# P times V of every fourth key tile as three f16 products: a fused attention and gated feed-forward kernel on one core

## The chip, the core and the metric

The kernel runs on one core of a Trainium2 chip. A core has five engines that run their own instruction streams and meet at semaphores: PE (TensorE, matrix products; its weight loads, PEld, are recorded apart), DVE (VectorE), ACT (ScalarE), POOL (GpSimd) and SP (SyncE, which here issues the DMAs). Products are written to PSUM, of which the kernel uses eight tiles of 128 x 512 f32 (banks); everything else lies in SBUF. The metric is the time of one execution in microseconds (us), the median of several runs.

## The reference

One block of an adaptive-layernorm transformer, S = 2048 rows, D = 512, 32 heads of 16, one shared key and value head, feed-forward width 1792, all in f32:

```python
mod = silu(c) @ w_mod                      # six rows of 512: sa, ca, ga, sb, cb, gb
h = layernorm(x) * (1 + ca) + sa
q = (h @ wq) as 32 heads of 16;  k = h @ wk;  v = h @ wv
p = softmax(q k^T / 4);  o = p @ v
x = x + ga * (o @ wo)
h = layernorm(x) * (1 + cb) + sb
x = x + gb * (((h @ w_gate) * (h @ w_up)) @ w_down)
```

## The kernel before, in words

**f32 through f16.** Most f32 matrices are kept as two f16 halves, hi and lo, with t = hi + lo: `hi` is t converted, `lo` is t - hi. A product of two such matrices is three f16 products, hi*hi, lo*hi and hi*lo (`TERMS`). Before the change, P times V is the one large product that is still done in f32.

**Tiling.** The rows are cut into 8 blocks of 256 (`ST`), the heads into 4 groups of 8 (`NC`). A block with a head group is a *unit* (`u`, 0 to 31; four units are one *superblock* `sb` of rows). The keys are cut into 16 tiles of 128 (`kt`). For a unit and a key tile, four tiles P of 128 keys x 512 (two heads' queries each, numbered by `p` and `a`) come from four score products (`qk_exp`, L648) and four exponentials on ACT (L661). `pv` (L665) multiplies them with the key tile's V, 128 x 32 (16 values, 16 ones that give the softmax's denominator), as four f32 products side by side in four column groups of 32. This is a *burst*. All 16 key tiles of a unit add up in one PSUM bank, which `pv_out` (L673) evicts. Then `normalise` (L681) brings the sums back over DMAs, and Pool multiplies (L706) and splits the result (L708, L709) for the output projection.

**The maxima.** The softmax needs each row's maximum before its exponentials. For the next unit, score products (L601) go to PSUM and DVE reduces them (L605), 64 a unit.

**The side work.** All other matrix products are *side groups* (`Group`, L511): query projections, output projection (`wo_work`), gate and up (`ffn_work`, 14 groups a superblock, 24 halves of two 256-column products each) and down (2 groups, 84 halves each). A half uses 64 of the 128 rows of PE, so it runs beside a score or maximum product on the other 64 rows. A gate-up group is finished by ACT (`g`, L847), DVE (`gf`, L849) and Pool, which writes the two halves of `glu` (L850, L851).

**The order.** Nothing is scheduled by a planner: `attend` (L1218) writes the program out in turns, two turns for two key tiles. In the side-work style `MANY` a turn is

```python
MANY = "x1 e0 x1 m0 x1 e0 x1 e0 x1 m0 x1 m0 x1 m0 x1 e0"
```

x a side half, e a score product with its exponential, m a maximum product. In the first of the two turns e makes the tiles with `a` = 0 of both key tiles, in the second those with `a` = 1. `end_turn` (L1229) closes a turn: it emits the finishing of side groups that ended in it, the eviction of a unit, then the burst of the key tile before, then `hooks` (L1278), which steps the weight preparation and, at four places of a unit (`NORM_AT`), the normalisation. On each engine the instructions stand in the order in which they are written there.

The two row halves of a side group add into one PSUM bank, so a half may only follow a half of the other rows when that one is done. The program ensures it with a wait of the first half of a turn for the last exponential of the turn before, on ACT (`sync`).

Of the kernel before, what the change touches and what calls it, by code (L numbers as in the profile page):

```python
# [23 lines left out]
ST = 256  # L24
# [10 lines left out]
SLOTS = (0, 1, 2, 3, 6, 7)  # L35
# [5 lines left out]
NORM_AT = (5, 12, 15, 19)  # L41
NBANK = 8
QPRE = 24
# [20 lines left out]
def adaln_mqa_glu_kernel(ctx: ExitStack, tc: tile.TileContext, x_in, wq_in, wk_in, wv_in, wo_in,  # L64
# [37 lines left out]

    c4 = consts.tile([KC, 128], F32, name="c4")
# [11 lines left out]
    for i in range(6, 8):  # L115
        xts.append([work.tile([128, D], F32, name="P", tag="P", bufs=8) for _ in range(2)])
# [12 lines left out]
    hf3 = [work.tile([128, BT], F32, name="P", tag="P", bufs=8) for k in range(KC)]  # L129
# [96 lines left out]
    ssqs = [kwb[:, 2 * n * BT:2 * n * BT + 2 * F].bitcast(F32) for n in (KC, 2 * KC)]  # L226
    kng = kwb[:, 2 * NHF * BT:2 * NHF * BT + BT]
# [86 lines left out]
    def v_mm(b):  # L314
        p = ps_hold("pvt", (128, 4, 16))
        for i in range(4):
            nc.tensor.matmul(p[:, i, :], parts[b][:, i * 128:(i + 1) * 128], lane[:, 16:32], start=True, stop=True)

        def out():
            nc.scalar.activation(vst[:, 4 * b:4 * b + 4, 0:16], p, AF.Copy, scale=inv[:, 0:1] if b else 1.0)  # L320
            ps_give(p)
        posts.append(out)
# [48 lines left out]
    kb = consts.tile([128, 8], F32, name="kb")  # L371
    inv = consts.tile([128, 3], F32, name="inv")
# [15 lines left out]
    nc.gpsimd.tensor_scalar(sckb, sck, inv[:, 0:1], 0.0, op0=OP.mult, op1=OP.add)  # L388
    combine(0, selk)
# [9 lines left out]
    evs = consts.tile([128, 1], F32, name="evs")  # L399

    def ev_scales():

        t = work.tile([128, 2], F32, name="evt", bufs=1)
        nc.vector.tensor_reduce(evs, ident.rearrange("p (a r) -> p a r", a=4)[:, :, 0:16], axis=AX.XY, op=OP.add)
        nc.vector.reciprocal(t[:, 0:1], kb[:, 5:6])
        nc.gpsimd.tensor_tensor(t[:, 0:1], t[:, 0:1], evs, op=OP.mult)
        nc.gpsimd.tensor_scalar(t[:, 1:2], evs, -1.0, 1.0, op0=OP.mult, op1=OP.add)
        nc.gpsimd.tensor_tensor(evs, t[:, 0:1], t[:, 1:2], op=OP.add)

# [43 lines left out]
    def last_rows():  # L453
# [21 lines left out]
             15: lambda: h_halves(1, KA), 17: lambda: h_halves(1, KB), 20: ev_scales}  # L475
# [6 lines left out]
    sync = {"due": False, "exp": None, "before": None}  # L482
    pending = []

    def flush():
        for f in pending:
            f()
            sync["due"] = True
        pending.clear()

    class Group:
# [31 lines left out]
        def half(self, r):  # L523

            mm = self.put(r, r + 1)
            if self.rows not in (None, r):
                tc.add_manual_dep(mm.ins, sync["before"], SYNC)
            self.rows, self.turn, sync["due"] = r, now[0], True
            if self.ended():
                ended.append(self)  # L530
# [89 lines left out]
    def max_fin(u):  # L620
        mms[u] = work.tile([128, 2, 8], F32, name="mm")
        nc.vector.tensor_reduce(mms[u], mparts[u], axis=AX.X, op=OP.max)

# [18 lines left out]
    pvb = {}  # L642
    ptl = {}
    oc = {}
# [3 lines left out]
    def qk_exp(u, kt, p, a, last=False):  # L648
        s = sst[u % 3]
        ptl[u, kt, p, a] = work.tile([128, D], F32, name="P", tag="P", bufs=8)  # L650
        t = ps_sc()
        keys = kst[64 * a:64 * a + 50, kt * 128:(kt + 1) * 128]
        if pending and last:
            for c in range(2):
                if c:
                    flush()
                nc.tensor.matmul(t[:, c * ST:(c + 1) * ST], keys, s[64 * a:64 * a + 50, c, p, :], start=True, stop=True)  # L657
        else:
            nc.tensor.matmul(t.rearrange("k (c n) -> k c n", c=2), keys, s[64 * a:64 * a + 50, :, p, :],  # L659
                             start=True, stop=True)  # L660
        ex = nc.scalar.activation(ptl[u, kt, p, a], t, AF.Exp)  # L661
        if sync["due"]:
            sync.update(due=False, exp=ex.ins.name)

    def pv(u, kt):  # L665
        if kt == 0:
            pvb[u] = ps_hold("pv")
        for j in range(4):
            p, a = divmod(j, 2)
            nc.tensor.matmul(pvb[u][32 * j:32 * j + 32, :], vst[:, kt, :], ptl[u, kt, p, a],  # L670
                             start=(kt == 0), stop=(kt == KT - 1))

    def pv_out(u):  # L673
        sb, ch = divmod(u, NC)
        ev = work.tile([128, BT], F32, name="ev", tag="ev", bufs=3)
        nc.scalar.activation(ev, pvb[u], AF.Copy, scale=evs)
        ps_give(pvb[u])
        pd[u] = dram.tile([128, BT], F32, name=f"pd{u}")
        nc.sync.dma_start(pd[u], ev)
# [48 lines left out]
    def load_x(t):  # L728
        if t < KT - 2:
            x1s[t] = work.tile([128, D], F32, name="x1", tag="x1", bufs=6)  # L730
        else:
            x1s[t] = work.tile([128, D], F32, name="x1p", tag="P", bufs=8)
        nc.sync.dma_start(x1s[t], x_rows[t * 128:(t + 1) * 128, :])
# [58 lines left out]
    def ln2_work(sb):  # L792
        st = {}

        def tr(i):
            def f():
                if not h2s:
                    h2T = big.tile([128, 2, 2, KC, ST], F16, name="h2T", tag="wq")
                    glus.append(big.tile([128, 2, 2, FT, ST], F16, name="glu", tag="big"))
# [32 lines left out]
    def ffn_work(sb):  # L832

        def glu():
            return glus[0][:, sb % 2]
# [57 lines left out]
    def late_weights():  # L893
# [37 lines left out]
        def stage(n):  # L931
            if "d" in W:
                t = work.tile([128, D], F32, name="wsl", tag="xl", bufs=3)
            else:
                t = hfs[:, SLOTS[taken[0] % len(SLOTS)], :]
# [237 lines left out]
    side = deque(wlist)  # L1173
# [43 lines left out]

    def attend(u, kt):  # L1218
# [7 lines left out]
        orders = [[(w[0], int(w[1:] or 0)) for w in s.split()] for s in (style if style is NO_SIDE else (style, style))]  # L1226
        count = {}

        def end_turn(kt):  # L1229
# [3 lines left out]
            for f in ends:  # L1233
                f()
            ends.clear()
# [11 lines left out]
        for turn in range(2):  # L1247
            now[0] = u * NSTEP + 2 * (kt + turn)
            sync["before"] = sync["exp"]
            drain_posts()  # L1250
            order = orders[turn]
            for j, (what, a) in enumerate(order):
                if j == len(order) // 2:
                    drain_posts()
                    if style is not NO_SIDE:
# [22 lines left out]
    def hooks(u, i):  # L1278
# [5 lines left out]
        if u > 0 and i in NORM_AT:  # L1284
            if i == NORM_AT[0]:
                nrm[:] = normalise(u - 1)
            nrm[NORM_AT.index(i)]()
        if i == 20 and u > 0 and u % NC == 0:
# [25 lines left out]
    pv(u, KT - 1)  # L1314
    pv_out(u)
# [61 lines left out]
```

## Time and profile before

| | |
|---|---|
| median of 3 runs | 1664.51 us (1664.37 to 1664.66) |
| span of the profiled execution | 1663.8 us |
| instructions recorded | 39821 |
| attention, first to last burst | 79.5 us to 1551.2 us (starts) |
| after it, the rest of the side work and the last superblock | to 1663.8 us |

The profile is of one execution. Its page gives busy times by engine, the chain of work that ended last, and groups of instructions: a line of the kernel, engine, operation, what it writes and reads, shape and count, then busy time and mean ns of one, then the idle time ahead of it and what ended that. L511 is line 511 of the kernel before. The trace also gives instructions in order of time, with start and duration in us; neighbours of one kind are merged there (x4), and what an engine waited for stands in brackets. Stretches of time give for each engine the busy us and the number of instructions.

### The profile page before, as it was taken

How to read it: one execution, taken by the hardware profiler on the slowest of the kernel's cores; microseconds unless marked ns; L12 is line 12 of the kernel's file. 1: busy time of each engine (PE TensorE's matmuls, PEld its weight loads, DVE VectorE, ACT ScalarE, POOL GpSimd, SP SyncE). 2: the span in 40 equal slices, each digit the busy share in tenths (PEclk: the TensorE clock that was granted, in tenths of full speed). 3: DMA queues.
4: the chain of work that ended last, by engine and by line, in shares of the span. 5: the costliest groups of instructions: out<-in, count | busy, mean ns of one | idle time of the engine just before them, and what ended most of it. 6: DMA issues, size and time to landing. Idle time of an engine off the chain costs nothing.

```text
span 1663.8 us, 39821 instructions
## 1 busy us (share of the span) xinstructions
PE 1643.3 (99%) x15677; PEld 747.1 (45%) x15677; DVE 1402.3 (84%) x2434; ACT 1234.8 (74%) x2389; POOL 523.5 (31%) x833
## 2 busy tenths in 40 slices
PE   8899999999999999999999999999999999999999
PEld 4333333355533554335543355434545345454776
DVE  7999999998998999899998999999998999980211
ACT  5688888888777877777877787777878777877300
POOL 4857537864841111301112011300113001210322
PEclk9999999999999999999999999999999999999999
DMA  6313313342210001000000000000000000000100
GB/s 237 108 59 100 95 43 120 96 129 80 77 51 24 18 12 32 19 32 20 20 26 23 25 13 24 26 25 26 20 29 15 26 22 20 26 14 21 33 13 14
DMA packets 66024, 75.39 MB, mean 45 GB/s; under 512 B 17702, under 2 KB 46634, under 8 KB 65836
## 3 DMA queue, kind: packets, MB, share of 16 engines
q1 hardware_dynamic: 63724, 72.26, 13.7%
q8 instruction: 123, 2.02, 0.5%
q10 hardware_dynamic: 2112, 0.59, 0.1%
q14 instruction: 65, 0.53, 0.1%
HBM read 55.51 MB, written 17.04 MB: 44 GB/s over the span
## 4 chain that ended last, share of the span: by engine, by line
PE 93%; ACT 2%; DVE 2%; DMA 1%; issue 1%; POOL 0%; SPq 0%; ACTq 0%; DVEq 0%
PE side L511 41%; PE pv L670 30%; PE mx L601 8%; PE sc L659 8%; PE sc L657 3%; ACT P L661 2%; DVE mpart L605 1%; DMA xbig<-in_A_x_dram 1%; PE mx L805 1%; PE mxt L629 0%; ACT hf L813 0%; PE sc L601 0%; DVE bs L248 0%; DMA kwb<-in_B_w_down_dram 0%; DMA wkv<-in_A_wv_dram 0%
## 5 line engine op out<-in xcount | busy, mean ns | idle before, releaser
L605 DVE TENSOR_REDUCE mpart<-mx 128x1 f32<-128x512 f32 x2016 | 1274.1, 684 | 104.0 <-PE mx L601 95.7
L661 ACT ACTIVATE P<-sc 128x512 f32<-128x512 f32 x2048 | 1094.8, 598 | 274.2 <-PE sc L659 226.9
L601 PE MATMUL mx<-kst,sst 48*128 48x512 f16 x2032 | 631.5, 377 | 3.8 <-ACT P L661 1.7
L659 PE MATMUL sc<-sst,kst 50*128 50x512 f16 x1792 | 597.5, 379 | 0.6 <-ACT P L661 0.3
L670 PE MATMUL pv<-P,vst 128*32 128x512 f32 x4096 | 545.3, 605 | 0.7
L511 PE MATMUL side<-h2T,wg 64*128 64x256 f16 (+1 forms) x2396 | 540.8, 271 | 0.1
L511 PE MATMUL side<-h2T,wu 64*128 64x256 f16 (+1 forms) x2396 | 538.7, 270 | 0.0
L511 PEld LDWEIGHTS <-wg 64*128 64x128 f16 (+1 forms) x2396 | 226.0, 94 | 230.5 <-ACT P L661 194.0
L511 PE MATMUL side<-wd,glu 64*128 64x512 f16 (+1 forms) x1172 | 272.8, 378 | 0.2 <-ACT P L661 0.2
L850 POOL TENSOR_SCALAR glu<-gf 128x256 f16<-128x256 f32 x112 | 45.8, 409 | 671.3 <-DVE gf L849 583.9
L511 PEld LDWEIGHTS <-wu 64*128 64x128 f16 (+1 forms) x2396 | 226.4, 94 | 43.0 <-issue 7.8
L601 PEld LDWEIGHTS <-sst 48*128 48x128 f16 x2064 | 189.9, 94 | 34.2 <-issue 17.4
L659 PEld LDWEIGHTS <-kst 50*128 50x128 f16 x1792 | 162.9, 94 | 63.0 <-issue 50.3
L511 PEld LDWEIGHTS <-glu 64*128 64x128 f16 (+1 forms) x1172 | 98.5, 94 | 192.4 <-ACT P L661 85.9
L670 PEld LDWEIGHTS pv<-P,vst 128*32 128x32 f32 x4096 | 80.7, 108 | 160.9 <-issue 150.1
L849 DVE TENSOR_TENSOR gf<-side,g 128x256 f32<-128x256 f32 x112 | 46.7, 418 | 79.8 <-ACT g L847 77.7
L657 PE MATMUL sc<-sst,kst 50*128 50x256 f16 x512 | 96.9, 268 | 0.1
L511 PE MATMUL side<-h,wq 64*128 64x512 f16 (+1 forms) x372 | 95.0, 376 | 0.4 <-ACT P L661 0.4
L847 ACT ACTIVATE g<-side 128x256 f32<-128x256 f32 x112 | 42.3, 379 | 65.6 <-PE side L511 65.3
L511 PE MATMUL side<-wo,och 64*128 64x512 f16 (+1 forms) x360 | 86.3, 377 | 0.0
L851 POOL TENSOR_TENSOR glu<-gf,glu 128x256 f16<-128x256 f32 x112 | 75.3, 673 | 9.3
L706 POOL TENSOR_TENSOR oc<-oc,rr 128x256 f32<-128x256 f32 x31 | 22.7, 731 | 146.6 <-DMA rr<-ri 100.4
(233 smaller groups left out, 865.4 us busy)
## 6 DMA issues: line engine op xcount, KB each, us to landing
pd<-ev SPq DMA_DIRECT2D x32, 256.0 KB
kwb<-in_B_w_gate_dram SPq DMA_DIRECT2D x32, 224.0 KB
kwb<-in_B_w_up_dram SPq DMA_DIRECT2D x32, 224.0 KB
sst<-qd SPq DMA_DIRECT2D x180, 32.0 KB
qd<-q SPq DMA_DIRECT2D x16, 256.0 KB
oc<-pd SPq DMA_DIRECT2D x64, 64.0 KB
rr<-ri SPq DMA_DIRECT2D x64, 64.0 KB
x<-in_A_x_dram SPq DMA_DIRECT2D x14, 256.0 KB
```

The source lines that it names most:

```text
L511: return nc.tensor.matmul(self.p[:, c * w:(c + 1) * w], left[rows], right[rows], start=start and c == 0, stop=stop and c == len(terms) - 1)
L601: nc.tensor.matmul(m, s[64 * a:64 * a + 48, t // 2, p, t % 2 * 128:(t % 2 + 1) * 128], w[64 * a:64 * a + 48, :], start=(i == 0), stop=(i = ...
L605: nc.vector.tensor_reduce(part, m, axis=AX.X, op=OP.max)
L657: nc.tensor.matmul(t[:, c * ST:(c + 1) * ST], keys, s[64 * a:64 * a + 50, c, p, :], start=True, stop=True)
L659: nc.tensor.matmul(t.rearrange("k (c n) -> k c n", c=2), keys, s[64 * a:64 * a + 50, :, p, :], start=True, stop=True)
L661: ex = nc.scalar.activation(ptl[u, kt, p, a], t, AF.Exp)
L670: nc.tensor.matmul(pvb[u][32 * j:32 * j + 32, :], vst[:, kt, :], ptl[u, kt, p, a], start=(kt == 0), stop=(kt == KT - 1))
L706: eng.tensor_tensor(o, o, st["r"], op=OP.mult)
L847: nc.scalar.activation(g, p[:, 0:ST], AF.Copy, scale=2.0 ** -45)
L849: nc.vector.tensor_tensor(gf, p[:, ST:2 * ST], g, op=OP.mult)
L850: nc.gpsimd.tensor_scalar(glu()[:, 0, f, :], gf, 1.0, 0.0, op0=OP.mult, op1=OP.add)
L851: nc.gpsimd.tensor_tensor(glu()[:, 1, f, :], gf, glu()[:, 0, f, :], op=OP.subtract)
```

## The change

1. From unit 9 on (when the weight preparation on Pool, `side_items`, has run out), every fourth key tile (`EVERY`) is marked in `split_p`, but for the last two of each superblock's first unit and the first of its second. 76 key tiles are marked.
2. The four P tiles of a marked key tile are written by ACT to a region of their own (`p_split`), and Pool makes the f16 halves of each with a conversion and a subtraction (`p_halves`). They are emitted one P tile at a time: at the end of the key tile's first turn, in the middle and at the end of its second, and in the middle of the next turn. V of these key tiles is split once (`v16`).
3. The burst of a marked key tile comes two turns later than it did (`P_LAG`) and holds twelve f16 products in place of four f32 ones.
4. So that each turn still has one burst, one ready key tile is held back (`ready_p`): the order of key tiles in a unit's sum changes, one turn in unit 9 has no burst, and one burst is left for the end.
5. Ahead of the last exponential of a turn with an f16 burst, ACT makes a 1x1 copy that waits for the last side half; the next turn waits for that copy instead of the exponential.
6. P is scaled by 2^14 for the range of f16 (`P_BIAS` is taken off the maxima by a new 128x16 DVE instruction), V's scale is applied when V is evicted, and the eviction of a unit no longer scales (`evs` is gone).
7. Room: twelve P buffers in place of eight; `glu` has one buffer in place of two; four new P buffers and the split region lie behind it. Two staging slots move (`SLOTS`). The normalisation's places are counted from the unit's eviction (`out_at`).

```diff
-SLOTS = (0, 1, 2, 3, 6, 7)
+SLOTS = (0, 1, 2, 3, 12, 13)
-NORM_AT = (5, 12, 15, 19)
+NORM_AT = (2, 9, 12, 16)
+EVERY = 4
+P_LAG = 2
...
     def max_fin(u):
         mms[u] = work.tile([128, 2, 8], F32, name="mm")
         nc.vector.tensor_reduce(mms[u], mparts[u], axis=AX.X, op=OP.max)
+        nc.vector.tensor_scalar(mms[u], mms[u], -P_BIAS, None, op0=OP.add)
...
+        if (u, kt) in split_p:
+            ptl[u, kt, p, a] = None, p_split[0][:, 2 * a + p]
+            todo_p.append((p, a))
...
+        if last and sync["early"]:
+            ex = nc.scalar.activation(tok[:, 1:2], tok[:, 0:1], AF.Copy)
+            tc.add_manual_dep(ex.ins, sync["half"], SYNC)
+            sync.update(due=False, exp=ex.ins.name)
...
+    def p_halves():
+        if todo_p:
+            p, a = todo_p.popleft()
+            t, (hi, lo) = p_split[0][:, 2 * a + p], [p_split[1][:, 2 * a + p, h] for h in range(2)]
+            nc.gpsimd.tensor_scalar(hi, t, 1.0, 0.0, op0=OP.mult, op1=OP.add)
+            nc.gpsimd.tensor_tensor(lo, t, hi, op=OP.subtract)
...
     def pv(u, kt):
...
+        if (u, kt) in split_p:
+            terms = [(v16[:, vl, kt // EVERY, :], [p_split[1][:, 2 * a + p, pl] for p, a in heads])
+                     for vl, pl in ((0, 0), (1, 0), (0, 1))]
+        else:
+            terms = [(vst[:, kt, :], [t for _, t in parts])]
+        for n, (v, ps) in enumerate(terms):
+            for j in range(4):
+                nc.tensor.matmul(pvb[u][32 * j:32 * j + 32, :], v, ps[j], start=start and n == 0,
+                                 stop=stop and n == len(terms) - 1)
...
+    def split_due(v):
+        return bool(late_p) and v - late_p[0] >= P_LAG
+
+    def pv_turn(v):
+        if divmod(v, KT) in split_p:
+            late_p.append(v)
+        else:
+            ready_p.append(v)
+        if split_due(v):
+            pv(*divmod(late_p.popleft(), KT))
+        elif ready_p:
+            pv(*divmod(ready_p.popleft(), KT))
...
         def glu():
-            return glus[0][:, sb % 2]
+            return glus[0]
...
+        calm = not (u % NC == 0 and kt >= KT // 2 or u % NC == 1 and kt == 0)
+        if style is MANY and kt % EVERY == 0 and p_split and not side_items and calm:
+            split_p.add((u, kt))
...
         def end_turn(kt):
             for g in ended:
                 g.finish()
...
+            p_halves()
             v = u * KT + kt - 1
             if v >= 0:
-                pv(*divmod(v, KT))
-                if v % KT == KT - 1:
-                    ends.append(lambda: pv_out(u - 1))
+                pv_turn(v)
```

How the order of instructions moves. First PE at a turn's end while gate-up groups run: the last score product of the turn, the burst, and the first side half of the next turn. Before (`vst` is V in f32):

```order
L657 MATMUL sc<-sst_130,kst 128x256
L670 MATMUL pv<-P,vst 32x512 x3
L670 MATMUL pv<-P,vst 32x512 [waits Activation_49]
L511 LDWEIGHTS wg [waits Activation_49]
L511 MATMUL side<-h2T,wg 128x256
```

In the changed kernel, at the burst of a marked key tile (`v_341` is `v16`, `glu` the tensor in which the split region lies; the rows left out are the products in between, with a weight load each):

```order
L672 MATMUL sc<-sst_128,kst 128x256
L708 LDWEIGHTS v_341
L708 MATMUL pv<-glu,v_341 32x512 [waits Pool_49]
...
L708 MATMUL pv<-glu,v_341 32x512
...
L708 MATMUL pv<-glu,v_341 32x512 [waits Pool_49]
L512 LDWEIGHTS wg [waits Activation_49]
L512 MATMUL side<-h2T,wg 128x256
```

The burst now waits for Pool at its first, second, fourth and twelfth product, and the side half behind it for ACT as before (for the 1x1 copy).

Second, Pool while gate-up groups run. Before, it has one pair of instructions for a gate-up group, and one normalisation a unit:

```order
L850 TENSOR_SCALAR glu<-gf 128x256 [waits DVE_49]
L851 TENSOR_TENSOR glu<-gf,glu 128x256 [waits Pool_49]
L706 TENSOR_TENSOR oc<-oc,rr 128x256 [waits DMAHW3_49,DMAHW4_49,DMAHW1_49,DMAHW0_49]
L708 TENSOR_SCALAR och<-oc 128x256 [waits PE_49,Pool_49]
L709 TENSOR_TENSOR och<-oc,och 128x256 [waits Pool_49]
```

In the changed kernel the pairs of the split (L688, L689) stand between them:

```order
L913 TENSOR_SCALAR glu<-gf 128x256 [waits DVE_49]
L914 TENSOR_TENSOR glu<-gf,glu 128x256 [waits Pool_49]
L688 TENSOR_SCALAR glu<-glu 128x512 [waits Activation_49]
L689 TENSOR_TENSOR glu<-glu 128x512 [waits Pool_49]
L688 TENSOR_SCALAR glu<-glu 128x512 [waits Activation_49,Pool_49]
L689 TENSOR_TENSOR glu<-glu 128x512 [waits PE_49,Pool_49]
L913 TENSOR_SCALAR glu<-gf 128x256 [waits DVE_49]
L914 TENSOR_TENSOR glu<-gf,glu 128x256 [waits Pool_49]
L688 TENSOR_SCALAR glu<-glu 128x512 [waits Activation_49]
```

The two pairs in the middle are the third and fourth of a marked key tile, behind a gate-up group that ended in its second turn; the pair that begins in the last row is the first of the next marked key tile, behind a group that ended in its first turn.

Third, Pool in the second unit of a superblock, where the layernorm's rows are normalised on Pool (`n`, L769 before, L822 now). Before, the two stand behind their variances with a gate-up product and a normalisation between; now the second one stands between the third and the fourth pair of a marked key tile:

```order
L688 TENSOR_SCALAR glu<-glu 128x512 [waits Activation_49,Pool_49]
L689 TENSOR_TENSOR glu<-glu 128x512 [waits Pool_49]
L822 TENSOR_SCALAR n_18264<-x_17849,st_18018,ry 128x512
L688 TENSOR_SCALAR glu<-glu 128x512 [waits Activation_49,Pool_49]
L689 TENSOR_TENSOR glu<-glu 128x512 [waits PE_49,Pool_49]
```

More of the change, by code (lines that the diff above doesn't have):

```diff
@@ L100, in ps_misc, with p_tile @@
         return ps_mx("misc", shape)
+    def p_tile(n):
+        return work.tile([128, D], F32, name="P", tag=f"P{n}", bufs=1)
     c4 = consts.tile([KC, 128], F32, name="c4")
@@ L115, in adaln_mqa_glu_kernel @@
     for i in range(6, 8):
-        xts.append([work.tile([128, D], F32, name="P", tag="P", bufs=8) for _ in range(2)])
+        xts.append([p_tile(2 * (i - 6) + t) for t in range(2)])
     wqst = [work.tile([128, D], F32, name="wqst", tag="gf", bufs=4) for k in range(KC)]
@@ L128, in adaln_mqa_glu_kernel @@
         nc.sync.dma_start(wqst[k], wq_in[k * 128:(k + 1) * 128, :])
-    hf3 = [work.tile([128, BT], F32, name="P", tag="P", bufs=8) for k in range(KC)]
+    hf3 = [p_tile(4 + k) for k in range(KC)]
     wq = big.tile([128, 2, KC, D], F16, name="wq", tag="wq")
@@ L481, in adaln_mqa_glu_kernel @@
     ended = []
-    sync = {"due": False, "exp": None, "before": None}
+    sync = {"due": False, "exp": None, "before": None, "half": None, "early": False}
     pending = []
@@ L527, in half @@
                 tc.add_manual_dep(mm.ins, sync["before"], SYNC)
-            self.rows, self.turn, sync["due"] = r, now[0], True
+            self.rows, self.turn, sync["due"], sync["half"] = r, now[0], True, mm.ins.name
             if self.ended():
```

96 lines of the change are left out of this document (65 added, 31 removed).

## The prediction

> **What bounds the kernel now.** I read the page's busy shares and its chain of waits first, then the stretches of 100 us, then single turns in order of time, last the groups by line.
>
> ```profile
> PE 1643.3 (99%) x15677; PEld 747.1 (45%) x15677; DVE 1402.3 (84%) x2434; ACT 1234.8 (74%) x2389; POOL 523.5 (31%) x833
> ...
> PE 93%; ACT 2%; DVE 2%; DMA 1%; issue 1%; POOL 0%; SPq 0%; ACTq 0%; DVEq 0%
> ```
> ```profile
> core 0: 1663.8 us, clock 0.998
> ```
> ```profile
> 1000.00:1100.00 100.00, 99.85 (x1020) 45.84 (x1016) 91.92 (x156) 78.86 (x152) 22.91 (x40) 1.00 0.08 23
> 1100.00:1200.00 100.00, 99.96 (x1005) 44.44 (x1005) 91.95 (x155) 78.45 (x150) 10.02 (x18) 1.00 0.07 23
> ```
>
> The columns of the stretches are PE, PEld, DVE, ACT, POOL, then the granted clock. PE is never idle, at full clock, and the chain runs along it for 93%; DVE, at 92%, is next; Pool has 77 to 90 us of every 100 free. A busy PE is not yet a PE that cannot be quicker, so I look at single turns (one turn: 8 halves of a side group, 4 maxima, 4 scores, one burst of P times V):
>
> ```profile
> 999.65 0.28 PE L511 MATMUL side<-h2T,wg 64*128 64x256 f16 x1
> 999.77 0.27 PE L511 MATMUL side<-h2T,wu 64*128 64x256 f16 x1
> ...
> 1000.08 2.25 ACT L661 ACTIVATE P<-sc 128x512 f32<-128x512 f32 x4 [0.65 <-PE sc L659]
> ...
> 1001.56 0.16 PEld L670 LDWEIGHTS pv<-P,vst 128*32 128x32 f32 x8 [0.21 <-issue]
> 1001.56 1.06 PE L670 MATMUL pv<-P,vst 128*32 128x512 f32 x8
> 1002.23 0.38 ACT L847 ACTIVATE g<-side 128x256 f32<-128x256 f32 x1
> 1002.56 0.28 PE L511 MATMUL side<-h2T,wg 64*128 64x256 f16 x1
> ...
> 1002.75 0.42 DVE L849 TENSOR_TENSOR gf<-side,g 128x256 f32<-128x256 f32 x1
> ...
> 1003.25 0.40 POOL L850 TENSOR_SCALAR glu<-gf 128x256 f16<-128x256 f32 x1 [7.46 <-DVE gf L849]
> 1003.74 0.67 POOL L851 TENSOR_TENSOR glu<-gf,glu 128x256 f16<-128x256 f32 x1
> ...
> 1004.41 1.06 PE L670 MATMUL pv<-P,vst 128*32 128x512 f32 x8
> ...
> 1007.26 1.06 PE L670 MATMUL pv<-P,vst 128*32 128x512 f32 x8
> ...
> 1010.18 1.06 PE L670 MATMUL pv<-P,vst 128*32 128x512 f32 x8
> ```
>
> Bursts start 2.85, 2.85 and 2.92 apart. A burst holds PE 1.00 (1001.56 to 1002.56), the sixteen 256-column products of the side group at 0.11 each the other 1.85. PE sets the turn, and whatever stops PE inside a burst is paid in full.
>
> **The change part by part.** *The burst.* A burst holds four f32 products side by side, each recorded as two (4096 for 2048):
>
> ```profile
> L670 PE MATMUL pv<-P,vst 128*32 128x512 f32 x4096 | 545.3, 605 | 0.7
> L670 PEld LDWEIGHTS pv<-P,vst 128*32 128x32 f32 x4096 | 80.7, 108 | 160.9 <-issue 150.1 <-ACT P L661 9.9 <-DVE mpart L605 0.4
> L659 PE MATMUL sc<-sst,kst 50*128 50x512 f16 x1792 | 597.5, 379 | 0.6 <-ACT P L661 0.3
> ```
>
> A recorded half is about 0.22 longer than an f16 product of the same 512 columns, so it streams twice and the burst is four streams of 0.22; the remaining 0.13 of its 1.00 is entry and exit. As three f16 rounds it is 0.78. The order of the instructions has 76 such bursts (912 f16 products), so 76 x 0.218 = 16.6 us are saved if nothing waits. Bounds: 0 (below, third rival) to 0.34 a burst (entry and exit vanish too), 0 to 26 us. I take 0.218; four heads' streams at f16 move as many bytes per us as at f32.
>
> The eight weight loads of the f32 burst lie in its first 0.16 us, under its first round. The Trainium skill ("TensorE: Matmul & The Clock Gate", Part 3, the mechanism) says that a weight load overlaps running products only where their row groups differ, which here they do not; by that rule the loads of rounds two and three would stand in the open and the gain be near nothing. This trace disagrees, with that 0.16.
>
> *Pool's split.* Each of a split key tile's four P tiles takes one conversion and one subtraction, 128x512, of the kinds in the first two rows:
>
> ```profile
> L818 POOL TENSOR_SCALAR h2T<-hf 128x512 f16<-128x512 f32 x14 | 8.6, 617 | 35.3 <-ACT hf L813 31.5 <-PE side L511 3.8
> L819 POOL TENSOR_TENSOR h2T<-hf,h2T 128x512 f16<-128x512 f32 x14 | 16.3, 1163 | 1.2
> L769 POOL TENSOR_SCALAR n<-x,st,ry 128x512 f32<-128x512 f32 x8 | 16.7, 2084 | 0.0
> ```
> ```profile
> 1073.90 0.62 POOL L818 TENSOR_SCALAR h2T<-hf 128x512 f16<-128x512 f32 x1
> 1074.60 1.17 POOL L819 TENSOR_TENSOR h2T<-hf,h2T 128x512 f16<-128x512 f32 x1
> ...
> 1237.23 0.23 POOL L210 TENSOR_SCALAR rv<-st 128x1 f32<-128x1 f32 x1 [11.59 <-DVE st L760]
> ...
> 1239.02 0.19 POOL L215 TENSOR_TENSOR ry<-ry,rt 128x1 f32<-128x1 f32 x1
> ```
>
> With 0.08 between instructions a pair is 1.95, a key tile 7.8 us, 593 us over 76 key tiles. In four turns (11.4 us) Pool has room: 7.8, and 1.24 every third turn for the gate-up product (0.40 + 0.67, two gaps). But Pool works in order, and the burst has a due time. Count from B, the start of the burst that ends the split key tile's first turn. Its f16 burst stands three turns on, at B+8.55; its last round begins 0.44 later, and the last product needs the fourth tile's low half at B+8.99. The first two exponentials end at B-0.9 and B-0.4 (the ACT row: 1000.08, four in 2.25), and for the other two heads at B+2.0 and B+2.5. Pool could thus be ready at B-0.9+7.8 = B+6.9. What spoils this is the gate-up product, which ends every third turn and, as its rows show, can start on Pool only at B+1.69 of its turn (1003.25 against 1001.56), after g and gf; in Pool's order it stands ahead of the split's instructions that follow it. Key tiles come every fourth turn, so in 12 turns three cases occur:
> - it ends in the split's first turn: all four pairs start behind it, at B+1.69+1.24 = B+2.93, and end at B+10.7; PE waits 1.7.
> - in the second turn: two pairs behind it, from B+4.54+1.24 = B+5.78 to B+9.7; PE waits 0.7.
> - in the third: nothing, as the four pairs are ahead of it.
>
> That is 2.4 us lost for 0.65 gained per 12 turns of gate-up work. In the down and output projections nothing is lost. I walked Pool's whole order for all 76 with these prices (other rows at their means, each row no earlier than its operand): 37 in time, 16 late by 0.4 to 0.9 (10 us together), 18 by 1.4 to 1.9 (30), and 5 in the units in which a block's rows are normalised, where L769's 2.08 or the variance chain (L210 to L215, 1.98) stands between a split's pairs, by 2.9 to 4.7 (20). Sum 60 us. Bounds: with pairs 10% shorter the same walk gives 38; with pairs at what half as many columns cost (L850, L851: 1.24 with gaps), 7.
>
> What is queued behind PE's wait: the whole next turn. ACT and DVE then catch up, and turns of 2.92 return to 2.85 for a turn or two: 39 stalls x 0.1 = -4 us.
>
> *The 1x1 copy on ACT* ahead of the last exponential of an f16 turn. It lets the next turn's products go before that exponential ends.
>
> ```profile
> L634 ACT ACTIVATE mt<-mxt 16x128 f16<-16x128 f32 x32 | 8.5, 267 | 15.0 <-PE mxt L629 15.0
> L622 DVE TENSOR_REDUCE mm<-mpart 128x16 f32<-128x64 f32 x32 | 7.0, 220 | 1.1
> ```
> ```profile
> PEld mx L956 <- POOL kwb L946: 2.5, 1, 2.5
> ```
>
> At most 0.27 x 76 = 20 us of ACT, covered by its 0.65 idle at each turn's start; uncovered, the saving would shrink by as much. DVE's new 128x16 subtraction (32 times; L622, the nearest row, takes 0.22) lies in its 8% idle; uncovered 7 us.
>
> *The reserve* lets one turn early in unit 9 go without a burst and puts one burst behind the last turn: -0.3 (that turn is left to DVE, 92% busy) and +1.0. The later normalisation moves with its data. Single glu buffer: the down products that read it precede the writes on PE, 0. Staging slots and the value scales (units 0 to 8): 0, where PE's longest wait for staged weights is that 2.5 us; at most it is gone. Twelve P buffers instead of eight: 0.
>
> Sum, against the profiled execution: 1663.8 - 16.6 + 60 - 4 + 1 = 1704.2. The median of the runs lies 0.7 above the span, so **1705 us**.
>
> **The rivals.**
> 1. *Pool keeps pace* (the other side): no stall, only the gain, 1664.5 - 16.6 + 1 = 1649. It decides where a pair falls to (8.99 - 2.93)/4 = 1.51 us. For it: the profile's page warns that Pool's spans are rough, and Pool's mean load leaves room. Against: the spacing of L818 and L819 is made of start times, and the conversions are the same size and type.
> 2. *Half the stalls*: pairs of about 1.6 us (the walk's stalls then equal the gain), or gate-up products that arrive earlier because the stalls give ACT and DVE time. The time would be 1664.
> 3. *The f16 burst is no shorter*: two more sets of weight loads in the open, 2 x 0.11 a burst as L670's loads are 0.11 each, or DVE at 92% keeps the turn at 2.85. 16.6 us are lost beside the stalls: 1721. The 0.16 above speaks against it. By the rule of the Trainium skill named above, this one comes.
> That the change does not do what it says is excluded by the order of instructions.
>
> **How the numbers follow.** Forecast 0.68, first rival 0.15, second 0.07, third 0.10. The forecast's own range, from the stall sum of 38 to 65 us and the gain's bounds, is 1683 to 1718. Holding 8 in 10 needs the second rival and most of the third: 1660 to 1720. A measurement here tells 0.2%, 3.3 us. Faster: the first rival and a part of the second, 0.17; within 0.2%: 0.05; slower: forecast, third rival and the rest, 0.78.
>
> **What would show it.** In the profile after: f16 bursts of 0.78 where Pool is early; where a gate-up product precedes the four pairs, a PE wait for Pool's L689 of about 1.7 inside the burst, and 0.7 where it stands between them; some 55 to 60 us of such waits in all; Pool's rows L688 and L689 at 617 and 1163 ns. Wrong, if these rows are clearly shorter, if bursts start on time with PE not waiting for Pool, or if the f16 bursts take 1.00 in stages without gate-up work.

## The result: 2.7% slower

The changed kernel takes 1709.33 us (median of 4 runs, 1707.82 to 1711.67), the kernel before 1664.59 (4 runs). The ratio is 1.0267, 95% interval 1.0254 to 1.0280. The profiled execution has a span of 1709.8 us against 1663.8, so 46.0 us are to be explained.

The page of the changed kernel, its busy shares and its chain of waits:

```profile
PE 1654.8 (97%) x15981; PEld 757.2 (44%) x15981; DVE 1410.4 (82%) x2465; ACT 1235.8 (72%) x2465; POOL 1063.2 (62%) x1442
...
PE 84%; POOL 6%; DVE 5%; ACT 3%; issue 2%; DMA 1%; POOLq 0%; ACTq 0%; SPq 0%; DVEq 0%
```

Pool's busy time has doubled from 523.5 us, and Pool, which had no share in the chain, has 6% of it (some 100 us). The same two stretches as before (PE, PEld, DVE, ACT, POOL, granted clock) show PE with gaps, and a clock that is no longer full:

```profile
1000.00:1100.00 100.00, 97.33 (x1078) 49.31 (x1073) 92.56 (x160) 77.83 (x156) 56.06 (x79) 1.00 0.07 22
1100.00:1200.00 100.00, 98.11 (x945) 39.92 (x946) 87.79 (x146) 75.33 (x152) 73.86 (x91) 0.98 0.07 22
```

The groups of the f16 bursts and of Pool's pairs (busy us, mean ns, then the idle time before them and its releaser):

```profile
L689 POOL TENSOR_TENSOR glu<-glu 128x512 f16<-128x512 f32 x304 | 352.6, 1160 | 25.3
L688 POOL TENSOR_SCALAR glu<-glu 128x512 f16<-128x512 f32 x304 | 188.7, 621 | 111.0 <-ACT glu L680 66.4
L708 PE MATMUL pv<-glu,v 128*32 128x512 f16 x912 | 80.8, 385 | 31.1 <-POOL glu L688 15.6
```

The 912 f16 products are there, the pairs cost what their nearest rows said (617 and 1163), and PE stood 31 us inside the bursts. (That is less than the bursts' lengthening below: a recorded product lasts 0.38 us where the next round may follow 0.22 after its start, so the first part of a gap looks busy. A burst's length shows the gap whole.)

A late burst of the kind that the prediction called its first case, in order of time:

```profile
561.27 0.41 POOL L913 TENSOR_SCALAR glu<-gf 128x256 f16<-128x256 f32 x1 [3.96 <-DVE gf L912]
561.76 0.67 POOL L914 TENSOR_TENSOR glu<-gf,glu 128x256 f16<-128x256 f32 x1
562.40 0.62 POOL L688 TENSOR_SCALAR glu<-glu 128x512 f16<-128x512 f32 x1
...
568.25 0.62 POOL L688 TENSOR_SCALAR glu<-glu 128x512 f16<-128x512 f32 x1
568.96 1.16 POOL L689 TENSOR_TENSOR glu<-glu 128x512 f16<-128x512 f32 x1
```
```profile
568.22 0.40 PE L708 MATMUL pv<-glu,v 128*32 128x512 f16 x3
568.92 0.62 PE L708 MATMUL pv<-glu,v 128*32 128x512 f16 x8 [0.31 <-POOL glu L688]
570.16 0.38 PE L708 MATMUL pv<-glu,v 128*32 128x512 f16 x1 [0.62 <-POOL glu L689]
570.47 0.28 PE L512 MATMUL side<-h2T,wg 64*128 64x256 f16 x1
```

The burst before it began at 559.6. Pool waits 3.96 us for the gate-up operand with the split's first tiles behind it, starts the product 1.7 after that burst's start, as forecast, then four pairs without a gap. PE begins at 568.22, does three products, and stands for the fourth tile's two halves. The burst lasts 2.25 (568.22 to 570.47) instead of 0.76.

I measured all 76 f16 bursts so, from their first product to PE's next other product: 39 take 0.76 to 0.81; 14 take 1.05 to 1.40; 17 take 1.59 to 2.39; 5 take 3.42 to 4.78. The 76th is the kernel's last. It is on time too: two f32 bursts stand directly behind it, and the first of them begins 0.66 after it. So 40 are on time. Over 0.76 the late ones have 7.3, 23.7 and 17.9, together 48.9 us.

### The profile page after: what moved, and what is told of

The parts are those of the page before. It is cut to its first block, busy times and chain, and to the rows that moved or that the text cites. A ratio compares the mean times of both kernels' runs of the same rounds, so it can differ in the third digit from the quotient of the medians.

```text
span 1709.8 us, 41661 instructions
## 1 busy us (share of the span) xinstructions
PE 1654.8 (97%) x15981; PEld 757.2 (44%) x15981; DVE 1410.4 (82%) x2465; ACT 1235.8 (72%) x2465; POOL 1063.2 (62%) x1442
## 4 chain that ended last, share of the span: by engine, by line
PE 84%; POOL 6%; DVE 5%; ACT 3%; issue 2%; DMA 1%; POOLq 0%; ACTq 0%; SPq 0%; DVEq 0%
PE side L512 38%; PE pv L708 26%; PE mx L602 8%; PE sc L674 8%; DVE mpart L606 4%; POOL glu L689 3%; PE sc L672 3%; POOL glu L688 2%; ACT P L680 1%; ACT glu L680 1%; DMA xbig<-in_A_x_dram 1%; PE mx L868 1%; PE mxt L631 0%; DVE bs L255 0%; PE sc L602 0%
## 5 line engine op out<-in xcount | busy, mean ns | idle before, releaser
L680 ACT ACTIVATE P<-sc 128x512 f32<-128x512 f32 x1281 | 707.7, 599 | 143.9 <-PE sc L674 104.3
L680 ACT ACTIVATE glu<-sc 128x512 f32<-128x512 f32 x767 | 429.7, 596 | 158.4 <-PE sc L674 113.7
L708 PE MATMUL pv<-P,vst 128*32 128x512 f32 x2562 | 454.9, 606 | 0.7
L689 POOL TENSOR_TENSOR glu<-glu 128x512 f16<-128x512 f32 x304 | 352.6, 1160 | 25.3
L708 PE MATMUL pv<-glu,vst 128*32 128x512 f32 x926 | 303.1, 605 | 0.2
L688 POOL TENSOR_SCALAR glu<-glu 128x512 f16<-128x512 f32 x304 | 188.7, 621 | 111.0 <-ACT glu L680 66.4
L708 PEld LDWEIGHTS pv<-P,vst 128*32 128x32 f32 x2562 | 65.6, 108 | 106.4 <-issue 97.8
L708 PE MATMUL pv<-glu,v 128*32 128x512 f16 x912 | 80.8, 385 | 31.1 <-POOL glu L688 15.6
```

Source lines behind the costliest of these rows:

```text
L680: ex = nc.scalar.activation(ptl[u, kt, p, a][1], t, AF.Exp)
L688: nc.gpsimd.tensor_scalar(hi, t, 1.0, 0.0, op0=OP.mult, op1=OP.add)
L689: nc.gpsimd.tensor_tensor(lo, t, hi, op=OP.subtract)
L708: nc.tensor.matmul(pvb[u][32 * j:32 * j + 32, :], v, ps[j], start=start and n == 0, stop=stop and n == len(terms) - 1)
```

## The experiments

Each run has the kernel before timed beside it on the same chip: 1665.94 for the first four, 1665.50 for the next four, 1665.98 for the next three, 1666.12 for the last. Ratios are to that. Line numbers move by a few with each edit.

**1. No split.** Key tiles are never put on the list, so the rest of the change stands alone.

```diff
-            split_p.add((u, kt))
+            pass
```

> No key tile is split: all bursts are f32 again, Pool has no pairs and ACT no 1x1 copy; the single glu buffer, the larger P pool, the value scales, the later normalisation and the reserve's code stay. My theory (the loss is PE waiting for Pool's pairs, plus what the rest of the change costs in units 0 to 8): before + the 4.6 us by which the changed kernel is already late at the start of unit 9, so about 1669. Rival A (the rest of the change costs nothing, the early loss is chance): 1665. Rival B (the rest of the change is where the 45 us went): about 1690 or more.

Measured: 1672.11, ratio 1.0039 (1.0024 to 1.0053). The profile's span is 1671.0, 7.2 above before: 5.5 of that by the start of unit 9 (a unit is counted from its first exponential), the rest in steps between -0.25 and +0.42 a unit. So the parts that I had put at nothing cost 6 to 7 us. One of them is seen at once, in DVE's row order at the start:

```profile
21.88 0.16 DVE L400 RECIPROCAL vsc<-kb 128x1 f32<-128x1 f32 x1 [0.82 <-POOL kb L388]
21.96 0.98 DVE L268 TENSOR_SCALAR xbig<-xbig,st,ry 128x512 f32<-128x512 f32 x2
```

The new reciprocal waits for Pool, and the row normalisation behind it (L268, before the change L261) starts at 21.96 instead of 21.02.

**2. The f16 burst without Pool.** ACT writes a split tile's P as f16 at once; the low half is left out, and the third round reads the same tile again.

```diff
-            ptl[u, kt, p, a] = None, p_split[0][:, 2 * a + p]
-            todo_p.append((p, a))
+            ptl[u, kt, p, a] = None, p_split[1][:, 2 * a + p, 0]
...
-                     for vl, pl in ((0, 0), (1, 0), (0, 1))]
+                     for vl, pl in ((0, 0), (1, 0), (0, 0))]
```

> The split bursts stay f16 with three rounds, but ACT writes P straight as f16, the third round reads that same f16 tile again instead of the low half (the low half of P is left out, so the output loses precision), and Pool has no pairs. Measures the burst's gain alone. My theory: the first kernel of this set minus 76 x 0.22 to 0.24 = 17 to 18 us, about 1651. Rival A (DVE keeps the turn at 2.85, or the weight loads of rounds two and three stand in the open): no faster than the first of the set, about 1669. Rival B (half-clock stretches and small losses come with the f16 bursts themselves and not with the waits): 1655 to 1665.

Measured: 1653.12, ratio 0.9925 (0.9910 to 0.9940), 19.0 below run 1. Unit by unit against run 1, 1.3 of that was there at the start of unit 9, before any split; units 9 to 31 gave 17.6, or 0.23 a burst. The burst's group has no idle time:

```profile
L707 PE MATMUL pv<-glu,v 128*32 128x512 f16 x912 | 63.2, 382 | 0.0
```

So the gain is real and of the size worked out (0.218), neither DVE nor the weight loads take it back, and run 2 shows what the change would be worth if P came split for nothing.

**3. Pool's work beside.** The same 304 pairs at the same places, on a scratch area; all bursts f32.

```diff
+        if (u, kt) in side_p:
+            todo_p.append((p, a))
...
-            split_p.add((u, kt))
+            side_p.add((u, kt))
```

> Pool does the same 304 pairs at the same places of its order, on a scratch area that nothing reads; all bursts stay f32 and PE waits for no pair. Measures Pool's added load by itself. My theory (only the wait of the burst costs): within 4 us of the first of the set, about 1670, with what the gate-up product on Pool loses hidden. Rival (Pool's traffic slows DVE, ACT or PE, or its product comes late for the down projection): 1680 or more, with longer rows on DVE and ACT than in the first of the set.

Measured: 1695.99, ratio 1.0179 (1.0162 to 1.0196): 24 above run 1, so my theory that only the burst's own wait costs fell. But it is not a load on everything either. Unit by unit the loss sits in five places. 5.7 us, in unit 5, are the probe's own (a clearing of the scratch area that takes Pool 3.9 us). The others are units 17, 21 and 25 (5.6, 4.3 and 4.3) and 1.3 in unit 13; in most other units the difference is 0.0. DVE's reductions take 683 ns in both runs. In unit 17 the trace has

```profile
900.03 2.08 POOL L825 TENSOR_SCALAR n<-x,st,ry 128x512 f32<-128x512 f32 x1
...
902.16 0.90 PE L872 MATMUL mx<-ident,n 128*128 128x128 f32 x3 [2.92 <-POOL n L825]
```

Where a block's rows are normalised, Pool has the row work as well, and PE's transposes of the rows then wait for Pool in the pairs' stead. Those units have no room on Pool for the split, whichever is put first.

**4. The pair first.** At a turn's end the pair goes on Pool ahead of the gate-up product.

```diff
         def end_turn(kt):
+            p_halves()
             for g in ended:
...
-            p_halves()
             v = u * KT + kt - 1
```

> The changed kernel, but at a turn's end a split pair goes on Pool ahead of the gate-up product of the side group that has just ended, instead of behind it. My theory (the gate-up product ahead of the pairs makes the waits of about 1.5 us and 0.5 us): the 33 bursts that are late by 0.3 to 1.7 come down to near 0.78, some 30 us go; the five in the units where rows are normalised (17 us) stay, so about 1675 to 1682. Rival A (Pool is late by its load as a whole, whatever stands first): 1700 to 1710. Rival B (the waits only move to the product: the down projection then waits for glu): 1690 to 1705 with PE waiting for Pool's product rows.

Measured: 1689.22, ratio 1.0143 (1.0128 to 1.0158), 20.1 below the changed kernel. All bursts of the cases with a gate-up product are on time now, but for those in the units in which rows are normalised: 64 of 76 are on time. Twelve, at key tiles 4, 8 and 12 of these units, are late (up to 4.76), by 22.9 us together. (The texts on record of runs 5 and 11 count a thirteenth, the kernel's last, with 2.48 us, and 24.2 us in all. Those 2.48 are three bursts in a row, one f16 and two f32; they take 2.48 in run 2 as well, where nothing waits for Pool.) The waits of PE:

```profile
PE pv L708 <- POOL glu L688: 11.0, 5, 2.6
...
PE pv L708 <- POOL glu L689: 4.3, 9, 0.6
```

The changed kernel has 15.6 us in 18 waits and 15.2 in 32 there. No wait of PE for the gate-up product, which is now later, shows. The time came out 7 to 14 us above my range. I had left 17 us of waits in the row units where 22.9 stood, and I had not reckoned with half clock. Beginning shortly before the end of each of the five bursts of 3.6 us and more, the granted clock is 0.50 for 3.4 or 6.8 us, 30.7 us in all (17.1 in the changed kernel). The changed kernel shows it around its burst of 1290:

```profile
1289.99 0.40 PE L708 MATMUL pv<-glu,v 128*32 128x512 f16 x3
1292.78 0.62 PE L708 MATMUL pv<-glu,v 128*32 128x512 f16 x8 [2.39 <-POOL glu L688]
1294.02 0.59 PE L708 MATMUL pv<-glu,v 128*32 128x512 f16 x1 [0.63 <-POOL glu L689]
```
```profile
1290.00:1293.00 3.00, 0.61 (x9) 0.22 (x12) 1.59 (x4) 1.04 (x4) 2.92 (x4) 1.00 0.00 0
1294.00:1300.00 6.00, 5.98 (x38) 3.16 (x37) 2.58 (x4) 3.14 (x6) 5.58 (x9) 0.50 0.00 0
```

PE stands most of 4 us and then runs 6 us at half speed. The price follows unit by unit against run 2. Over units 9 to 31 the changed kernel is 56.4 us behind it, of which its f16 bursts are 48.7 longer than run 2's. Of the other 7.7, 5.5 are in the four units with half clock (17.1 us) and 2.1 in the nineteen without. Run 4 is 36.2 behind: 22.8 in bursts, 9.7 in the five units with half clock (30.7 us), 3.7 in the rest. Both give 0.32 us per us at half clock (in a part of which PE still stands). Unit 17 holds a long burst in both kernels. In the changed one no half clock follows it, and the unit is 3.9 longer with 4.0 in bursts; in run 4 it has 6.8 us of half clock and is 5.8 longer with 4.1 in bursts. What makes up the 2.1 and 3.7 of the other units is open.

**5. The pair first, and no split in those units.** Key tiles 4 and 8 of units 9, 13, 17, 21, 25 and 29 stay f32, and 64 split tiles remain. (These are the row units; the text on record calls them the first unit after a block's end, and they are the second.)

```diff
-        calm = not (u % NC == 0 and kt >= KT // 2 or u % NC == 1 and kt == 0)
+        calm = not (u % NC == 0 and kt >= KT // 2 or u % NC == 1 and kt <= 8)
```

> As the fourth run (pair ahead of the gate-up product), and besides key tiles 4 and 8 of the first unit after a block's end (12 of 76, where the normalising of rows stands on Pool) are not split. In the fourth run 13 bursts were late, 24.2 us in all, and every one but the last of the kernel was at key tile 4, 8 or 12 of these units; 30.7 us at half clock followed them, which with PE busy cost some 11 us. My theory (the row work on Pool is the whole of what is left): 1689 - 21 - 11 + 12 x 0.24 = about 1660, with no half-clock stretch after 480 us. Rival (Pool's load still costs elsewhere, as the scratch pairs of the third run did): 1668 or more.

Measured: 1660.36, ratio 0.9970 (0.9958 to 0.9982): faster than before, and where the theory had put it. No half clock after 480 us, no late burst (0.79 at most; the last is on time, as above), and

```profile
L708 PE MATMUL pv<-glu,v 128*32 128x512 f16 x768 | 53.2, 383 | 0.0
```

**6. A shorter pair.** The changed kernel's own order; of each pair only the subtraction, against a fixed tile.

```diff
-            nc.gpsimd.tensor_scalar(hi, t, 1.0, 0.0, op0=OP.mult, op1=OP.add)
-            nc.gpsimd.tensor_tensor(lo, t, hi, op=OP.subtract)
+            nc.gpsimd.tensor_tensor(lo, t, wo[:, 0, 0, :], op=OP.subtract)
...
-            terms = [(v16[:, vl, kt // EVERY, :], [p_split[1][:, 2 * a + p, pl] for p, a in heads])
+            terms = [(v16[:, vl, kt // EVERY, :], [p_split[1][:, 2 * a + p, 1] if pl else wo[:, 0, 0, :] for p, a in heads])
```

> The changed kernel in its own order (gate-up product first), all 76 key tiles split, but of each pair only the subtraction is done, against a fixed f16 tile; rounds one and two of the burst read that fixed tile, round three the subtraction's result (the conversion to the high half is left out, so the output is not P times V). A dose test of the pair's price: 1.24 us with its gap instead of 1.95. By the prediction's walk a pair under 1.51 lets all four end in time even behind the gate-up product (B+2.93+4x1.24 = B+7.9 against B+9.0), and the walk of all 76 gives 7 us of stalls: 1709 - 42 - some 6 of half clock = about 1661. Rival (the lateness is set by where Pool begins, by ACT's exponentials or by the wait itself, not by the pair's price): the waits shrink only by the share of the price, a third, and the time is 1690 or more.

Measured: 1657.71, ratio 0.9953 (0.9938 to 0.9968).

```profile
L688 POOL TENSOR_TENSOR glu<-glu,wo 128x512 f16<-128x512 f32 x304 | 344.7, 1160 | 163.8 <-ACT glu L680 163.7
...
L707 PE MATMUL pv<-glu,v 128*32 128x512 f16 x304 | 31.1, 379 | 1.2 <-POOL glu L688 1.2
```

Pool's pairs are a third shorter and the lateness does not shrink by a third; it goes almost whole, from 48.9 us to 2.9 (six bursts, all in the row units). That is a due time, as in the walk, and not a load. The walk had 7 us left.

**7. The value scale later.** Run 1 with the reciprocal and Pool's product behind it moved down a few lines, behind row work of DVE.

```diff
-    nc.vector.reciprocal(vsc[:, 0:1], kb[:, 5:6])
-    nc.gpsimd.tensor_tensor(vsc[:, 1:2], vsc[:, 0:1], inv[:, 0:1], op=OP.mult)
     combine(0, selk)
...
     ln_stats(4)
+    nc.vector.reciprocal(vsc[:, 0:1], kb[:, 5:6])
+    nc.gpsimd.tensor_tensor(vsc[:, 1:2], vsc[:, 0:1], inv[:, 0:1], op=OP.mult)
```

> The first run (no key tile split), with the value scale's reciprocal on DVE and its product on Pool moved behind DVE's next row work, where nothing of DVE waits for Pool. The reciprocal had waited 0.82 us for Pool and all of DVE with it. My theory (that wait is 0.9 us of the 6 us the rest of the change costs; the remainder is half-clock stretches and the new placement of early work): 1671 against 1672. Rival (that wait also sets the half-clock stretches and shifts behind it): 1666, no different from before.

Measured: 1669.69, ratio 1.0026 (1.0016 to 1.0035), against 1.0039 for run 1; the intervals overlap. The 0.9 us at 21 us is gone from the trace. Some 4 us of the rest remained.

**9. No scale on the maxima.** Run 7 without DVE's new 128x16 subtraction, which scales P by 2 to the 14.

```diff
-        nc.vector.tensor_scalar(mms[u], mms[u], -P_BIAS, None, op0=OP.add)
```

> The seventh run (no split, value scale moved) without DVE's extra 128x16 subtraction that scales P by 2 to the 14 (32 times; the output divides it out again). What the rest of the change still costs was 3 to 4 us there, 1.2 us of it in small steps over units 9 to 31. If the subtraction is that cost (DVE not covered): 1.2 to 2 us less, 1668. If DVE's idle covers it: 1670 as before.

Measured: 1664.87, ratio 0.9992 (0.9983 to 1.0001): no different from before, and 0.0034 (some 5 us) below run 7. So this one small instruction, 32 times, is most of what the rest of the change costs. (The change also sets `dynamic_dma_scratch_size` from 4096 to 256, which the list of the change leaves out. Run 9 has that too.) Run 7 against run 9, unit by unit, has steps of 1.04 in unit 2, 0.70 in unit 4 and 0.44 in unit 6, and the rest in small ones. The trace of run 7 in unit 2 (DVE, Pool, PE):

```profile
195.14 0.22 DVE L623 TENSOR_REDUCE mm<-mpart 128x16 f32<-128x64 f32 x1
195.40 1.02 DVE L624 TENSOR_SCALAR mm<-mm 128x16 f32<-128x16 f32 x1
...
195.26 1.13 POOL L1009 TENSOR_TENSOR kwb<-kwb 128x448 f32<-128x448 f32 x1
...
196.57 0.27 PE L631 MATMUL mxt<-ident,mm 128*16 128x128 f32 x1 [0.64 <-DVE mm L624]
```

The instruction takes 0.175 us in 24 of its 32 places and up to 1.02 in the others, and PE's transpose of the maxima waits for it.

**10. The old staging slots.** Run 7 with slots 6 and 7 in place of 12 and 13.

```diff
-SLOTS = (0, 1, 2, 3, 12, 13)
+SLOTS = (0, 1, 2, 3, 6, 7)
```

> The seventh run with the staged weights in slots 6 and 7 again instead of 12 and 13. If the new slots' order of loads makes the step of 1.05 us in unit 2 and 0.6 in unit 4: 1668. If not: 1670.

Measured: 1671.65, ratio 1.0033 (1.0021 to 1.0045). The slots are not the cause.

**8 and 11. Runs 5 and 7 together, and then one key tile less.** Run 8 has both edits; run 11 also leaves the last unit's key tile 12 unsplit:

```diff
-        calm = not (u % NC == 0 and kt >= KT // 2 or u % NC == 1 and kt <= 8)
+        calm = not (u % NC == 0 and kt >= KT // 2 or u % NC == 1 and kt <= 8 or u == NU - 1 and kt == 12)
```

> The fifth run with the value scale's reciprocal moved as in the seventh. If the two add up: the fifth run less what the seventh gains on the first, 1655 to 1660, below the kernel before. If the row work or Pool's load still costs, 1664 or more.

> The eighth run without the split of key tile 12 of the last unit, whose burst was the only late one left (2.48 us). Both ends of it are known: 1.7 us of wait go, 0.24 of gain go with them: 1658 against 1659.6, some 7 below the kernel before. If the wait only moves to the end's row work: 1660.

Measured: 1659.60, ratio 0.9968 (0.9956 to 0.9981), and 1660.69, ratio 0.9967 (0.9954 to 0.9979). Runs 5, 8 and 11 can't be told apart. Run 11 could not gain the 1.7 us that its text expected, because the last burst was not late (run 4), and the value scale's 0.9 does not show in the times. All three still have the subtraction of run 9.

**12. The scale in the exponential.** Run 8, with the scale as a per-partition bias of ACT's exponential in place of DVE's subtraction.

```diff
-        nc.vector.tensor_scalar(mms[u], mms[u], -P_BIAS, None, op0=OP.add)
...
-        ex = nc.scalar.activation(ptl[u, kt, p, a][1], t, AF.Exp)
+        ex = nc.scalar.activation(ptl[u, kt, p, a][1], t, AF.Exp, bias=pbias)
```

> The eighth run (pair first, 12 key tiles left out, value scale moved) with the scale of P by 2 to the 14 given to ACT's exponential as its bias instead of a subtraction on DVE. The ninth run took 4.8 us off by leaving that subtraction out; if it is the same 4.8 here and the biased exponential takes its 599 ns as before, 1659.6 - 4.8 = about 1655, some 11 below the kernel before. If a biased exponential is longer by 5% (2048 of them, ACT 75% busy), ACT is still covered and the time is the same; if the 4.8 us came from the early half-clock stretches and not from the subtraction, 1659 to 1660.

Measured: 1709.80, ratio 1.0263 (1.0249 to 1.0277), 50 us above run 8 and 55 above what I expected. The exponentials of run 8; then of run 12 the chain of waits, the exponentials and a stretch of 100 us:

```profile
L680 ACT ACTIVATE P<-sc 128x512 f32<-128x512 f32 x1313 | 725.8, 599 | 164.8 <-PE sc L674 124.5 <-PE mx L602 32.1 <-ACT P L680 0.8
```
```profile
PE 68%; ACT 24%; issue 5%; DVE 2%; DMA 1%; POOL 0%; ACTq 0%; SPq 0%; DVEq 0%
...
L681 ACT ACTIVATE P<-sc,pbias 128x512 f32<-128x512 f32 x1313 | 833.4, 690 | 109.3 <-PE sc L675 92.6
...
1000.00:1100.00 100.00, 98.89 (x1076) 49.13 (x1075) 92.11 (x156) 86.27 (x153) 48.43 (x72) 1.00 0.08 23
```

A biased exponential takes 690 ns, 15% more, not the 5% that I had allowed for. Bursts in 600 to 1500 us stand 2.99 apart (median) where run 8 has 2.85. On the mean over all 510 bursts it is 0.095 a turn, 48 of the 50 us. ACT is busy 86%, not 100, and yet has 24% of the chain (2% in run 8). The order of the program gives the likely reason: the first side product of a turn waits for the last exponential of the turn before, which is now up to 4 x 0.09 = 0.36 later. Whether the 5 us of run 9 are to be had in the fast version is open.

## Why the prediction was right

**The sum.** From the span before: +7.2 for the rest of the change (run 1), -17.6 for the gain in units 9 to 31 (run 2 against run 1), +48.7 for bursts longer than run 2's, +5.5 in the units with half clock and +2.1 in the others is 45.9 of the 46.0 us. The last two are remainders, so the sum closes by construction. That the 5.5 is the half clock rests on the same 0.32 us per us in run 4 and on unit 17; the 2.1 is unexplained.

**The burst, right.** 0.78 was forecast, 0.76 measured; -16.6 against -17.6. Of the third rival (a burst no shorter) nothing is left: run 2. With it falls, for this burst, the rule of the Trainium skill that the prediction weighed ("TensorE: Matmul & The Clock Gate", Part 3, the mechanism: weight loads overlap running products only in other row groups). With these loads in the open, at the prediction's 2 x 0.11, the burst would take 0.98; it takes 0.76. In the changed kernel's burst at 616.97 the loads of round two start 0.01 to 0.02 us and those of round three 0.23 to 0.24 us after the first product, while products of the round before run on the same rows.

**Pool's price and the due time, right.** 617 and 1163 ns forecast, 621 and 1160 measured. In the late burst above the last low half ends at 570.12, by the prediction's count of turns at B+10.5 where it said B+10.7. The first rival (Pool keeps pace) was to decide at 1.51 us a pair: at 1.95 Pool does not, at 1.24 (run 6) it does.

**The cases, right.** 37, 16, 18 and 5 bursts in the four classes were forecast, 40, 14, 17 and 5 counted, and run 4 shows that the gate-up product ahead of the pairs is the cause in 24 of the 31 bursts of the two middle classes: with the pair first they are on time, and the other seven stand in row units. **The size of the stalls was forecast at 60 and is 48.9**: the middle classes are late by 0.52 and 1.39 on average instead of 0.63 and 1.67, the five by 3.6 instead of 4.0. In the late burst above, 0.2 of this is the earlier end of the pairs and 0.07 the burst's own later start (B+8.62 for B+8.55). The second rival (half the stalls) came about a quarter of the way, 11 of its 41 us. **The relief of -4 did not come**: in the nineteen units without half clock the changed kernel is 33.9 behind run 2 and its bursts are 31.7 longer, so a stall cost its whole length.

**What the prediction missed.** That 1705 lies only 4 us from 1709 is in part luck, with errors of both signs. The stalls were 11 smaller and the gain 1 larger than forecast. Against that stand the relief of 4 that did not come, 6 more for the rest of the change (7.2 measured, 1 forecast), 5.5 at half clock and the 2.1 without a cause. The prediction's own range, 1683 to 1718, is also narrower than its bounds make it: 38 to 65 us of stalls and 0 to 26 of gain give 1674 to 1727. The two terms that it overlooked:
- *The edits at nothing.* The step was "DVE's new 128x16 subtraction lies in its 8% idle; uncovered 7 us". It is uncovered: 5 us (run 9). A share of idle time says nothing about an instruction that stands between the last maximum and the transpose for which PE waits. The value scales (units 0 to 8) were put at 0 with their wait for Pool overlooked: 0.9 us in the trace, a difference too small for the times to settle.
- *What comes after a long stall.* The five bursts in units with row work were forecast with their waits, 2.9 to 4.7, but as if PE went on at full speed. It did not, and that cost 5.5 us (run 4). The Trainium skill has the rule that I left out ("TensorE: Matmul & The Clock Gate", Part 1, What's actually happening): after an idle window of about 3.4 us the clock goes to half. The trace agrees in its units (stretches of 3.41 and 6.83 us), and after four of the five, though the waits were shorter than such a window (last section).

What stays open: the stretches at half clock in the first 150 us. Before has 6.8 us there, runs 1 and 3 have 13.7, run 7 has 6.8, run 9 has 10.2, and no edit accounts for it. At the 0.32 us per us found above, 6.9 us more or less of it would move a comparison by some 2 us (an estimate), so no difference of that size between two runs of this list is read as shown on its own.

## What to carry to other kernels

When work is moved to an engine with room, put its due time and what stands ahead of it in that engine's order first, and its share of busy time second: here 62% busy was late, and an order of two calls exchanged was worth 20 us. A split that is not worth its price in a few places (12 of 76) can turn the sign of the whole, so choose the places by what else the engine has to do there. A 128x16 instruction is not free because its engine has idle time, nor a bias because it needs no new instruction: both were the last thing before a wait.

## What the runs showed of the hardware that was not expected

**DVE's small subtraction waits for Pool's running instruction.** In run 7 it takes 174 to 177 ns in 24 places. In the other eight (391 to 1024 ns) a Pool instruction is running when it begins, and it ends 0.03 us after that one does: in the rows shown under run 9, at 195.40 + 1.02 = 196.42, Pool's at 195.26 + 1.13 = 196.39. In run 5, with the pairs on Pool, 19 of 32 are longer in this way. The Trainium skill ("GPSIMD Engine Reference", section 1, Specifications) says that the two share their SBUF interfaces, with contention for DVE instructions in a two-port mode or with two SBUF inputs. The trace agrees that there is contention; whether this instruction runs in such a mode, no run shows. The reductions from PSUM, by contrast, take 683 ns with and without the pairs beside them (runs 1 and 3).

**A per-partition bias makes ACT's 128x512 exponential 91 ns longer** (599 to 690; over all 2048 the mean rises by 91 as well). The Trainium skill has this price ("ScalarE: Activation LUTs", What ACT_TABLE_LOAD costs): about 93 ns for each pointer operand, and none for a bias given as an immediate. The trace agrees with the first; the second was not run.

**Half clock came from less than a whole idle window.** PE did eight products in the middle of the stall of 1290 us, and in run 3 a single wait of 2.92 us was enough. One of the changed kernel's five long bursts (906 us, 4.44) had none behind it, and none of its bursts up to 2.39 did.
